# Windows of 80 tokens in the product with v, one subtraction on GpSimd, fewer buffers

## The chip, the cores and the metric

The kernel runs on one core of a Trainium2 chip. The metric is device time in microseconds: the median of the runs, 788.82 us before (788.5 to 789.36, three runs). The profile is that of one execution. TensorE is called PE here, VectorE DVE, ScalarE ACT, GpSimd POOL, as in the profile.

## What is computed

Attention with two mixings of the heads, then two blocks of weights in float64:

```python
# q, k, v: (2, 12, 448, 64); w_pre, w_post: (12, 12)
scores = scale * np.matmul(q, k.transpose(0, 1, 3, 2))
scores = np.einsum('bhij,hg->bgij', scores, w_pre)
scores = scores - np.max(scores, axis=-1, keepdims=True)
attn = np.exp(scores)
attn = attn / (np.sum(attn, axis=-1, keepdims=True) + 1e-09)
attn = np.einsum('bhij,hg->bgij', attn, w_post)
attn = np.matmul(attn, v)
# x: (896, 768), the heads side by side
xn = x / sqrt(mean(x * x, -1) + 1e-6) * rms_g
x = (silu(xn @ w_gate) * (xn @ w_val)) @ w_out      # d_ff 1536
x = elu(x @ w_in2) @ w_out2                         # d_ff 2048
```

## The kernel before

Products that need float32's precision are made of parts: x = h + l, each exact in the format that PE takes. The weights' float64 words are turned into such parts on DVE and ACT (`convert`, L209 to L261), ahead of their use.

The attention works on one batch of 448 tokens after the other. The scores of a head go through DRAM (`s_d`) and come back as groups of ten tokens: 120 partitions hold (token, head), 448 columns the keys. There are 45 groups a batch, 90 in all, here numbered 0 to 89 through both. Each group goes through these steps, on the engine named:

- `g_split`, L468 and L469: high part on ACT, low part `sl` on POOL, for every other group;
- `g_premix`, L476 or L479 to L481: the first mixing of heads, PE;
- `g_max`, L488: the maximum, DVE, from PSUM; `g_exp`, L496: ACT, writes `e` and the sum;
- `g_sum`, L504, and `g_recip`, L511: DVE, one column;
- `g_high`, L524 on ACT or L526 on DVE: the normalised exponentials in float16, `eh`; `g_low`, L533, DVE: what is left of them, `el`;
- `g_postmix`, L554: the second mixing, PE, twelve matmuls with `eh` and `el` as the stationary operand, so that the result comes out with the keys on the partitions;
- `g_out`, L566: ACT copies it into `at`, the room of a window.

A window is some groups in a row. Once its last group has come through `g_out`, PE multiplies its `at` with v (L590), in five pieces, one beside each of the next groups. The result has the features on the partitions and the window's tokens as columns. Then a chain of ten pieces follows, one a step: `squares` (L596 on DVE makes `xt`; L603 to L606 square and add on POOL), `mean` (L612, PE), `root` (L619 on DVE, L623 on POOL), `diagonal` (L627, DVE), `spread` (L631, PE), `normed` (L634, DVE), `high` (L640, ACT, makes `xh`) and `low` (L643, makes `xl`). The last two windows of the second batch are `late`: their squares are made on ACT. `xh` and `xl` feed the first product with the weights.

The order is written out by hand. One loop has a step t for every group; in step t each engine gets, in this order, the work of different groups: on DVE the sum of group t-1, the maximum of t, the reciprocal of t-1, L533 of t-2, L526 of t-1; on PE the premix of t+1 and the postmix of t-3. Beside them stand q, k and scores of later heads, the windows' pieces and the chains' next piece, and near the end the conversion of the first two blocks of weights. So DVE reaches L533 of a group in the step after that in which PE got the postmix of the group two before.

A tile takes the room that its `bufs`-th predecessor of the same tag had, and the first writer waits until the readers of that one are done. Tags that the change touches are `eh` (L522), `el` (L532) and `xt` (L576).

## Time and profile before

| | before |
|---|---|
| median of the runs | 788.82 us |
| span of the profiled execution | 787.3 us |
| busy: PE, DVE, ACT, POOL | 759.4, 550.6, 445.6, 114.4 us |
| attention (to the last `xl` of the second batch) | about 294 us |

The profile gives for each engine the time in which it was busy. Matmuls are pipelined and the ends of their rows are modelled, so starts are the safer reading. PE is nearly full from 294 us to the end; before that different engines are full in different stretches.

### The profile page before, as it was taken

The page shows a single profiled execution, that of the slowest core. Times are in us where ns is not written, and L with a number is a line of the kernel's source. Part 1 is how long each engine was busy: PE and PEld are TensorE (multiplying, and loading weights), DVE is VectorE, ACT ScalarE, POOL GpSimd, SP SyncE. Part 2 cuts the span into 40 slices and gives each one's busy share as a digit, 9 for nine tenths or more (in the row PEclk, how much of TensorE's full clock was granted, in tenths as well). Part 3 has the DMA queues.
Part 4 walks back from the last instruction along what each step waited for, and adds up shares of the span by engine and source line. Part 5 has one row for each costly group of instructions (what it writes and reads, how often), then busy time and mean ns, then how long its engine had stood idle before and what let it go on. Part 6 is the DMA issues. An engine that isn't in the chain of part 4 may idle for free.

```text
span 787.3 us, 14708 instructions
## 1 busy us (share of the span) xinstructions
PE 759.4 (96%) x5655; PEld 673.1 (85%) x5655; DVE 550.6 (70%) x1135; ACT 445.6 (57%) x952; POOL 114.4 (15%) x141
## 2 busy tenths in 40 slices
PE   6779999999998999999999999999999999999997
PEld 5557778777776779999999999999999999999997
DVE  6356999665789938887877865652898887553651
ACT  7679888887987925654544433231576566221320
POOL 4212565333443400000000000000000000000000
PEclk9899999999998999999999999999999999999999
DMA  7798665668783303343332333231444343433512
GB/s 205 222 280 252 168 154 140 178 173 236 217 230 78 104 2 121 122 132 108 121 112 94 116 121 106 95 121 41 121 132 120 109 122 100 111 111 111 155 47 70
DMA packets 90249, 105.42 MB, mean 134 GB/s; under 512 B 16004, under 2 KB 86084, under 8 KB 90180
## 3 DMA queue, kind: packets, MB, share of 16 engines
q1 hardware_dynamic: 90180, 104.49, 46.0%
q8 instruction: 44, 0.72, 0.4%
q14 instruction: 25, 0.20, 0.1%
HBM read 82.46 MB, written 22.02 MB: 133 GB/s over the span
## 4 chain that ended last, share of the span: by engine, by line
PE 83%; DVE 7%; DMA 5%; ACT 2%; issue 1%; SPq 1%; POOL 1%; ACTq 0%; POOLq 0%
PE psa_t L197 13%; PE psa_t L198 13%; PE psa_t L199 13%; PE psv_t L590 5%; PE pst_t L554 4%; PE psf_t L198 4%; PE psf_t L199 4%; PE psf_t L197 4%; PE psa_t L966 3%; PE psa_t L964 3%; PE psa_t L965 3%; DMA s_d<-st 3%; PE psa_t L476 3%; DMA sg<-s_d 2%; PE psa_t L407 2%; DVE el L533 1%
## 5 line engine op out<-in xcount | busy, mean ns | idle before, releaser
L554 PEld LDWEIGHTS <-eh 120*112 120x112 f16 x720 | 66.8, 131 | 27.2 <-issue 21.8
L240 ACT ACTIVATE whl<-w 128x768 fp32r<-128x768 f32 x44 | 37.1, 844 | 86.0 <-PE psf_t L966 28.5
L244 ACT ACTIVATE whl<-w,g_sb 128x128 fp32r<-128x128 f32 x144 | 45.0, 393 | 64.1 <-PE psa_t L199 25.6
L219 ACT ACTIVATE w<-raw 128x768 f32<-128x768 f32 x68 | 62.5, 919 | 30.5 <-DVE whl L251 23.6
L469 POOL TENSOR_TENSOR sl<-sg,sh 120x448 fp32r<-120x448 f32 (+1 forms) x45 | 54.5, 1211 | 116.2 <-ACT sh L468 111.6
L251 DVE TENSOR_TENSOR whl<-w,whl 128x768 fp32r<-128x768 f32 x44 | 42.2, 958 | 41.1 <-ACT whl L240 40.0
L198 PE MATMUL psa_t<-x2l,whl 128*128 128x448 f32 x192 | 70.1, 365 | 0.0
L199 PE MATMUL psa_t<-x2h,whl 128*128 128x448 f32 x192 | 70.1, 365 | 0.0
L197 PE MATMUL psa_t<-x2h,whl 128*128 128x448 f32 x192 | 70.1, 365 | 0.0
L233 DVE SCALAR_TENSOR_TENSOR w<-w,raw 128x768 int32<-128x768 int32 x68 | 65.2, 958 | 2.3
L554 PE MATMUL pst_t<-m2h,eh 120*112 120x120 f16 x360 | 63.0, 217 | 2.7 <-ACT at L566 2.6
L227 DVE SCALAR_TENSOR_TENSOR raw<-raw 128x768 int32<-128x768 int32 x68 | 64.8, 953 | 0.0
L554 PE MATMUL pst_t<-m2h,el 120*112 120x120 f16 x360 | 63.1, 218 | 1.7 <-DVE el L533 1.7
L496 ACT ACTIVATE e<-psa_t,nmax 120x448 f32<-120x448 f32 (+1 forms) x90 | 58.0, 645 | 11.4 <-DVE rs L511 10.4
L533 DVE SCALAR_TENSOR_TENSOR el<-e,rs,eh 120x448 f16<-120x448 f32 (+1 forms) x90 | 64.0, 711 | 0.3 <-ACT eh L524 0.3
L554 PE MATMUL pst_t<-m2l,eh 120*112 120x120 f16 x360 | 63.0, 218 | 0.0
L488 DVE TENSOR_REDUCE nmax<-psa_t 120x1 f32<-120x448 f32 (+1 forms) x90 | 55.2, 613 | 8.4 <-PE psa_t L481 8.3
L197 PE MATMUL psa_t<-xh,whl 128*128 128x448 f32 x150 | 55.7, 372 | 1.0 <-ACT xh L640 1.0
L590 PE MATMUL psv_t<-at,vs 112*64 112x70 f32 (+3 forms) x1344 | 55.7, 230 | 0.0
L590 PEld LDWEIGHTS psv_t<-at,vs 112*64 112x64 f32 x1344 | 46.5, 139 | 9.9 <-issue 7.0
L198 PE MATMUL psa_t<-xl,whl 128*128 128x448 f32 x150 | 54.9, 366 | 0.0
L199 PE MATMUL psa_t<-xh,whl 128*128 128x448 f32 x150 | 54.8, 365 | 0.0
(167 smaller groups left out, 2059.2 us busy)
## 6 DMA issues: line engine op xcount, KB each, us to landing
raw<-in_moe_w_out_dram SPq DMA_DIRECT2D x28, 768.0 KB, 4.5
sg<-s_d SPq DMA_DIRECT2D x44, 420.0 KB, 5.0
s_d<-st SPq DMA_DIRECT2D x93, 196.0 KB, 3.2
raw<-in_moe_w_in_dram SPq DMA_DIRECT2D x16, 768.0 KB, 4.7
raw<-in_moe_w_gate_dram SPq DMA_DIRECT2D x12, 768.0 KB, 4.3
raw<-in_moe_w_val_dram SPq DMA_DIRECT2D x12, 768.0 KB, 4.4
vs<-in_v_dram SPq DMA_DIRECT2D x4, 672.0 KB, 7.7
kt<-in_k_dram SPq DMA_DIRECT2D x12, 224.0 KB, 3.8
```

Of the source, the lines that this page charges most:

```text
L197: nc.tensor.matmul(out=ps, lhsT=wh(kk), rhs=xh_(kk), start=(first and kk == 0), stop=False)
L198: nc.tensor.matmul(out=ps, lhsT=wh(kk), rhs=xl_(kk), start=False, stop=False)
L199: nc.tensor.matmul(out=ps, lhsT=wl(kk), rhs=xh_(kk), start=False, stop=(last and kk == nk - 1))
L219: nc.scalar.activation(out=w, in_=raw.bitcast(F32)[:, :, 1], func=ACTF.Copy, scale=REBASE)
L227: nc.vector.scalar_tensor_tensor(out=lo, in0=hi, scalar=SIGN, in1=lo, op0=ALU.bitwise_and, op1=ALU.bitwise_or)
L233: nc.vector.scalar_tensor_tensor(out=wi, in0=wi, scalar=3, in1=lo, op0=ALU.logical_shift_left, op1=ALU.bitwise_or)
L469: nc.gpsimd.tensor_tensor(out=sl[:r], in0=s32, in1=sh[:r].bitcast(F32), op=ALU.subtract)
L488: nc.vector.tensor_reduce(out=nmax[:r], in_=ps[:r, :S], axis=AXX, op=ALU.max, negate=True)
L496: nc.scalar.activation(out=e32[:r], in_=ps[:r, :S], func=ACTF.Exp, bias=nmax[:r], scale=1.0, accum_out=sm[:r])
L533: nc.vector.scalar_tensor_tensor(out=el[:r], in0=e32[:r], scalar=rs[:r], in1=eh[:r], op0=ALU.mult, op1=ALU.subtract)
L554: nc.tensor.matmul(out=o, lhsT=lhs[:r, c * CP:(c + 1) * CP], rhs=rhs[:r, :, :ni], start=(n == 0), stop=(n == 2),)
L590: nc.tensor.matmul(out=psx[s * D:(s + 1) * D, kk, :n], lhsT=vs[b][:, hh, c, :], rhs=at[:, c, hh, :n], start=(c == 0), stop=(c == NCH - 1),)
```

## The change

Windows now have eight groups (80 tokens), the last of each batch five (48 tokens); there are six a batch and not seven. `low` of a window runs on POOL, but for the two late windows. `eh` has three buffers and not four, `el` two and not three, `xt` two and not three. Comments are left out of the new code, with the lines kept.

```diff
@@ g_high, g_low
-            eh = ap.tile([GP, S], F16, tag="eh", name="eh", bufs=4)
+            eh = ap.tile([GP, S], F16, tag="eh", name="eh", bufs=3)
...
-            el = ap.tile([GP, S], F16, tag="el", name="el", bufs=3)
+            el = ap.tile([GP, S], F16, tag="el", name="el", bufs=2)
@@ windows
-        WGS = [[0, 7, 14, 21, 27, 33, 39, NG], [0, 7, 14, 21, 28, 34, 40, NG]]
+        WGS = [[0, 8, 16, 24, 32, 40, NG]] * B
         NW = len(WGS[0]) - 1
-        WMAX = 70
+        WMAX = 80
@@ window
-            xt = ap.tile([P, KD, WMAX], F32, tag="xt", name="xt", bufs=3)
+            xt = ap.tile([P, KD, WMAX], F32, tag="xt", name="xt", bufs=2)
...
             def low():
-                nc.vector.tensor_tensor(
+                (nc.vector if late else nc.gpsimd).tensor_tensor(
                     out=xl[:, :, tk], in0=xt[:, :, :n], in1=xh[:, :, tk].bitcast(F32), op=ALU.subtract
                 )
```

Tokens of the windows, and the groups (0 to 89) beside whose premix PE gets their five pieces:

| before: tokens | groups | after: tokens | groups |
|---|---|---|---|
| 70 | 12 to 16 | 80 | 13 to 17 |
| 70 | 19 to 23 | 80 | 21 to 25 |
| 70 | 26 to 30 | 80 | 29 to 33 |
| 60 | 32 to 36 | 80 | 37 to 41 |
| 60 | 38 to 42 | 80 | 45 to 49 |
| 60 | 44 to 48 | 48 | 50 to 54 |
| 58 | 50 to 54 | | |
| 70 | 57 to 61 | 80 | 58 to 62 |
| 70 | 64 to 68 | 80 | 66 to 70 |
| 70 | 71 to 75 | 80 | 74 to 78 |
| 70 | 78 to 82 | 80 | 82 to 86 |
| 60 | 84 to 88 | 80 (late) | behind 89 |
| 60 (late) | behind 89 | 48 (late) | behind 89 |
| 48 (late) | behind 89 | | |

DVE in the second batch, from `g_low` of group 68 on, shortly before the first block of weights is converted (L643 is `low`, L619 the start of `root`, L596 the first multiplication of a window). Before:

```order
L533 SCALAR_TENSOR_TENSOR el<-e_3969,rs,eh 120x448
L643 TENSOR_TENSOR xl<-xt,xh 128x6x70
L504 TENSOR_SCALAR sm<-sm 120x1
L488 TENSOR_REDUCE nmax<-psa_t 120x1
L511 RECIPROCAL rs<-sm 120x1
L533 SCALAR_TENSOR_TENSOR el<-e_4016,rs,eh 120x448
L526 TENSOR_SCALAR eh<-e_4048,rs 120x448
L619 TENSOR_SCALAR ms<-psa_t 70x1
```

After:

```order
L533 SCALAR_TENSOR_TENSOR el<-e_3881,rs,eh 120x448
L596 TENSOR_TENSOR xt<-psv_t,vsc 128x480
L504 TENSOR_SCALAR sm<-sm 120x1
L488 TENSOR_REDUCE nmax<-psa_t 120x1
L511 RECIPROCAL rs<-sm 120x1
L533 SCALAR_TENSOR_TENSOR el<-e_3931,rs,eh 120x448
L526 TENSOR_SCALAR eh<-e_3968,rs 120x448
L504 TENSOR_SCALAR sm<-sm 120x1
```

The subtraction L643 is gone from this queue; the window's first multiplication L596, which stood five steps further on, or two earlier for the window before, stands in its place.

POOL at the same place (L469 is `sl` of the premix, L603 to L606 the squares, L623 the root). Before:

```order
L623 TENSOR_TENSOR rstd<-ms,mhalf 70x1
L469 TENSOR_TENSOR sl<-sg,sh 120x448 x2
L603 TENSOR_TENSOR sq<-xt 128x420
L604 TENSOR_TENSOR sq<-sq 128x210
L605 TENSOR_TENSOR sq<-sq 128x70
L606 TENSOR_TENSOR sq<-sq 128x70
L469 TENSOR_TENSOR sl<-sg,sh 120x448 x2
L623 TENSOR_TENSOR rstd<-ms,mhalf 70x1
```

After:

```order
L606 TENSOR_TENSOR sq<-sq 128x80
L469 TENSOR_TENSOR sl<-sg,sh 120x448
L643 TENSOR_TENSOR xl<-xt,xh 128x6x80
L469 TENSOR_TENSOR sl<-sg,sh 120x448
L623 TENSOR_TENSOR rstd<-ms,mhalf 80x1
```

L643 now stands between two subtractions of the premix's parts, and ahead of the next root.

PE in the first batch, at group 42 (L554 is the postmix, L476 the next group's premix), where the old order had the last piece of a window of 60 tokens and the new one is between two windows:

```order
 L554 LDWEIGHTS el
 L554 MATMUL pst_t<-m2h,el 112x120
-L590 MATMUL psv_t<-at,vs 64x60 x8
 L476 MATMUL psa_t<-sg,m1f 120x448
 L554 LDWEIGHTS eh
```

The premix now follows the postmix directly.

## Rows read from the trace of the kernel before

**Rows 1.** The page's head: the length of the profiled execution.

```profile
span 787.3 us, 14708 instructions
```

**Rows 2.** Stretch, length, busy us of PE, PEld, DVE, ACT, POOL; clock, DMA, GB/s.

```profile
60.00:82.00 22.00, 21.94 (x246) 16.37 (x247) 15.23 (x45) 21.24 (x53) 5.38 (x6) 1.00 0.82 239
82.00:107.00 25.00, 22.10 (x285) 18.07 (x284) 24.30 (x55) 19.79 (x50) 17.18 (x21) 1.00 0.71 167
107.00:184.00 77.00, 76.84 (x1002) 60.71 (x1000) 59.13 (x166) 64.88 (x154) 34.08 (x41) 1.00 0.63 165
184.00:196.00 12.00, 11.44 (x132) 8.66 (x127) 6.98 (x20) 8.09 (x20) 3.52 (x5) 1.00 0.90 245
196.00:226.00 30.00, 30.00 (x354) 23.29 (x353) 22.00 (x64) 28.18 (x69) 12.90 (x16) 1.00 0.78 221
226.00:266.00 40.00, 36.90 (x487) 29.74 (x487) 39.55 (x97) 32.68 (x80) 17.48 (x19) 0.91 0.54 150
266.00:293.60 27.60, 26.56 (x401) 22.31 (x397) 13.78 (x41) 13.86 (x33) 6.07 (x9) 1.00 0.01 2
293.60:780.00 486.40, 486.35 (x2494) 458.79 (x2495) 338.39 (x571) 214.46 (x405) 0.00 (x0) 1.00 0.36 108
```

**Rows 3.** By line and form, count | busy us, mean ns: product with v.

```profile
L590 PE MATMUL psv_t<-at,vs 112*64 112x70 f32 x672 | 29.2, 234 | 0.0
```

**Rows 4.** Chain that ended last (start us, us, what): that product's pieces.

```profile
67.30 1.12 PE psv_t L590 x32
...
70.45 0.64 PE psv_t L590 x16
...
131.69 0.61 PE psv_t L590 x16
...
139.13 1.08 PE psv_t L590 x32
...
283.08 1.49 PE psv_t L590 x48
```

**Rows 5.** By line and form: spreading a window's norm.

```profile
L631 PE MATMUL psa_t<-dg,ones 70*128 70x70 f32 x14 | 2.7, 274 | 0.9 <-DVE sm L504 0.9
```

**Rows 6.** DVE's lines from 226 to 266 us.

```profile
L533 DVE SCALAR_TENSOR_TENSOR el<-e,rs,eh 120x448 f16<-120x448 f32 x15 | 11.2, 749 | 0.0
...
L255 DVE SCALAR_TENSOR_TENSOR whl<-w,g_sb,whl 128x128 fp32r<-128x128 f32 x12 | 5.3, 509 | 0.0
L526 DVE TENSOR_SCALAR eh<-e,rs 120x448 f16<-120x448 f32 x5 | 4.0, 796 | 0.0
...
L643 DVE TENSOR_TENSOR xl<-xt,xh 128x420 fp32r<-128x420 f32 x3 | 1.8, 584 | 0.0
L627 DVE TENSOR_SCALAR dg<-ident,rstd 70x70 f32<-70x70 f32 x2 | 1.4, 686 | 0.0
```

**Rows 7.** DVE in order of time: start us, us, instruction.

```profile
227.54 0.58 DVE L643 TENSOR_TENSOR xl<-xt,xh 128x420 fp32r<-128x420 f32 x1
228.05 0.14 DVE L504 TENSOR_SCALAR sm<-sm 120x1 f32<-120x1 f32 x1
```

**Rows 8.** By line and form: GpSimd's subtraction for the premix.

```profile
L469 POOL TENSOR_TENSOR sl<-sg,sh 120x448 fp32r<-120x448 f32 x44 | 53.3, 1212 | 110.7 <-ACT sh L468 106.2 <-PE psa_t L481 4.3
```

**Rows 9.** L526, L533 (min/median/max ns) and L255 over the run, one L627.

```profile
L526 DVE TENSOR_SCALAR eh<-e,rs x40: 439/449/2019, 40.9 to 250.7; 120x448 f16<-120x448 f32 x39, 96x448 f16<-96x448 f32 x1
...
L533 DVE SCALAR_TENSOR_TENSOR el<-e,rs,eh x90: 654/667/1232, 42.6 to 275.5; 120x448 f16<-120x448 f32 x88, 96x448 f16<-96x448 f32 x2
...
L255 DVE SCALAR_TENSOR_TENSOR whl<-w,g_sb,whl 128x128 fp32r<-128x128 f32 x144 | 43.8, 363 | 12.1 <-ACT whl L244 12.1
...
254.50 0.25 DVE L627 TENSOR_SCALAR dg<-ident,rstd 70x70 f32<-70x70 f32 x1
```

**Rows 10.** In order of time: one L533, and a postmix matmul.

```profile
250.08 0.67 DVE L533 SCALAR_TENSOR_TENSOR el<-e,rs,eh 120x448 f16<-120x448 f32 x1
...
249.87 0.31 PE L554 MATMUL pst_t<-m2h,el 120*112 120x120 f16 x1
```

## The prediction

> **What bounds the kernel now.** I read the busy time by stretch first, with cuts where the nearly full engine changes [rows 2]. From 293.6 us to 780 TensorE (PE) has 486.35 of 486.40 us: the three products with the weights, which the change doesn't touch and which simply start earlier or later. So everything is decided in the attention, up to 293.6 us. There the bound wanders. From 60 to 82 us ScalarE has 21.24 of 22 us. From 82 to 107 VectorE (DVE) has 24.30 of 25, while q and k of the second batch are prepared. From 107 to 184 and from 196 to 226 PE has all but 0.2 us. From 184 to 196 nobody is full: a DMA stall after v of the second batch is loaded. From 226 to 266 DVE has 39.55 of 40 us, because the first two blocks of weights are converted beside the groups; PE has 36.90, of which some at half clock (granted 0.91 on average, against 1.00 around it). From 266 to 293.6 PE has 26.56 of 27.6. A saving counts only where its engine is the full one: PE's in 107 to 226 and after 266, DVE's in 82 to 107 and 226 to 266. What ScalarE does is unchanged but for two copies of a window.
>
> **Product with v on PE.** A window is 48 products in the code, each two records, since 7 windows of 70 rows give 672 [rows 3]. They come in one piece of 32 records and four of 16. At 70 rows the pieces take 1.12 and 0.64 us, at 60 rows 1.08 and 0.61 [rows 4]; a window is 1.12 + 4 x 0.64 = 3.68, or 1.08 + 4 x 0.61 = 3.52. At 48 rows 48 records took 1.49, which is 31 ns a record and not less than at 60 rows (1.08 / 32 = 34, with a start-up of about 0.14 in it). [...] For 80 rows the bounds are the line through 60 and 70 (0.67 and 1.16, window 3.84) and everything in proportion to the columns (0.73 and 1.28, window 4.20). [...]
>
> All windows before: 7 x 3.68, four of 3.52, one of 60 rows in three long pieces (3.24), 58 rows 3.5, 48 rows 3.1: 49.7 us. After: nine of 4.09, one in three long pieces 3.75, 48 rows 3.45 and 3.1: 47.1. PE loses 2.6 us of work (3.8 to 1.5 at the bounds). But where? In PE's order, numbering the groups 0 to 89 through both batches, the premixes of groups 28 to 69 (the stretch to 226 us in which PE is full) had three pieces of 0.64, three windows of 3.52, one of 3.5 and two of 3.68 between them: 23.3. Now there are four windows of 4.09, one of 48 rows (3.45) and four pieces of the next (1.25 + 3 x 0.71 = 3.38): 23.2. Only 0.1 us falls out there, and one spread of the norm (L631, 2.7 / 7 = 0.39 us a window, [rows 5]), say 0.35. From group 85 on, four pieces of 0.61, 3.24 and 3.1 become two of 0.71, 3.75 and 3.1: 0.5 less. The other 2 us leave groups 16 to 27 and 70 to 84, where DVE is the full engine, and become idle time of PE. Sum for PE: **-1.0 us**.
>
> **The norm's chain on DVE, 226 to 266 us.** Three subtractions of the low part (L643) stand there, 0.58 us each, of which the next instruction sees 228.05 - 227.54 = 0.51 [rows 6, 7]. They leave DVE: -1.53. In DVE's order the 15 groups from 70 on also lose one of two multiplications by the norm (L634; same 420 elements, so 0.5), which now stands just behind the stretch; I count half, -0.25. Three operations that stay grow from 420 to 480 elements, 60 more at 1 ns (0.58 us for 420 bounds it at 1.4): +0.18. Together -1.6.
>
> Against it stand two of the moved subtractions, now on GpSimd (POOL). The nearest row is the subtraction of the premix's parts, 448 elements in 1212 ns [rows 8]; 480 elements make 1.30 us. POOL is busy 17.48 of the 40 us there [rows 2], and while it works DVE is slow: five L526 took 4.0 us where the median of one is 0.449, 15 L533 took 11.2 where it is 0.667, twelve L255 had a mean of 509 ns against 363 over the run, two L627 a mean of 686 where the shorter took 0.25 [rows 6, 9]. That is 1.8 + 1.2 + 1.8 + 0.9 = 5.7 us lost to 17.48 us of POOL, a third. Two times 1.30 by a third: +0.85. Bounds are nothing (0) and the whole 1.30 of each (+2.6). **-0.75 us**, between -1.6 and +1.0.
>
> **82 to 107 us.** By the order, groups 17 to 25 lose one L643 and gain one first multiplication of a window (xt), which has moved by a step: nothing. On average they must gain a little, 9 groups of 0.07; one subtraction on POOL falls on the end of the stretch. **-0.2 us**, between -0.7 and +0.6.
>
> **Fewer buffers.** With two buffers for el, the subtraction L533 of a group must wait until PE has done the postmix of the group two before; for eh the same wait stands one instruction later. In the trace this was nearly always over. I paired all 90: the one case in the DVE-bound stretches that would have waited is L533 at 250.08, where the last L554 of that postmix ends at 249.87 + 0.31 = 250.18 [rows 10]: 0.1 us. Premix and postmix stand back to back on PE, and DVE first takes the maximum of that premix, so the wait is met by construction; what would queue behind it on DVE is the next eh and the window's pieces. With two buffers of xt the older is read for the last time nine steps after it is written, and wanted again after thirteen or more. I count 0. **Tail:** the last window but one is 80 rows, not 60: four operations 60 to 120 elements longer before the last xl, **+0.2**.
>
> Sum: -1.0 - 0.75 - 0.2 + 0.2 = -1.75 us. The profiled span is 787.3 [rows 1], 1.5 us under the median of 788.82, which lies around the span; so 785.6 of span, **787.1 us**. A measurement of this kernel can tell about 0.2% (1.6 us) from no change, so the forecast sits just beyond that line.
>
> [...]
>
> **Rivals.** (1) *GpSimd blocks DVE in full.* Three moved subtractions lie where DVE is full (about groups 26, 71, 79). If each catches an L526 or a row of L255 it costs not a third but 1.3 to 1.57 us (2019 - 449), 3.9 to 4.7 together where I had counted 1.3; from 1.0 us each on the gain is gone, and from 1.55 on the kernel is measurably slower. With the worst, and 0.5 for a step elsewhere in which DVE is nearly full, 787.1 + 3.4 + 0.5 = 791. For it: the slow L526 rows. [...] (2) *Nothing arrives.* DVE's relief is eaten and PE's is idle time: 788.6. For it: the 2 us of PE work that fall out in the wrong stretches. (3) *More arrives.* DVE already loses 5.7 us to POOL from 226 to 266; the squares of the windows shift by one to seven steps and may leave the L255 rows alone, and a shorter stretch may spare PE the half clock: 2 to 3 us more, 784.5. (4) *The rings of el and eh couple DVE to PE.* If every group waits 0.3 us from 226 to 266, 15 x 0.3 = +4.5: 791.6. Against it, the paired times.
>
> **How the numbers follow.** Forecast (-0.5 to -3 us) 50%, of it 30 beyond -0.2%; more arrives 18%; nothing 15%; blocked 13%; rings 4%. Faster 0.48, same 0.35, slower 0.17. The range runs from 784.0 (the low ends of POOL's cost and half of rival 3) to 790.0 (POOL's upper end with the PE gain lost); beyond it lie some 2 in 10.
>
> **What would show it.** Right: from about 226 us a DVE-bound stretch shorter by about 1 us with no L643 in it, PE pieces of 0.71 and 1.25, L533 nearly never waiting for L554. Wrong: L526, L533 or L255 with larger means than before beside L643 on POOL; pieces under 0.68; a wait of L533 on PE; a DMA stall that grows, or a change after 293 us, which I exclude.

## The result, and the profile after

| | before | after |
|---|---|---|
| median of the runs | 788.82 us | 798.21 us (794.38 to 800.31, five) |
| profiled execution, and its span | span 787.3 us | 794.38 us, span 792.7 us |
| busy: PE, DVE, ACT, POOL | 759.4, 550.6, 445.6, 114.4 us | 756.7, 552.5, 444.8, 121.7 us |
| last `xl` written | 294.1 us | 299.3 us |
| from there to the end of the span | 493.3 us | 493.3 us |

The change is slower: 1.0109 times before, 95% interval 1.0083 to 1.0135. The forecast was 787.1 us, in a range from 784.0 to 790.0. In this document ratios leave out executions that are over 1.5% above the fastest of their kernel (three of the twelve of e1, one of e2, two of e3 below), and medians count them. The profiled execution is the shortest of the five and explains only the 5.3 us by which its attention ends later. A second profile of the same kernel, of an execution of 801.24 us (h0 below), ends its attention at 298.8 us and then takes 500.7 us instead of 493.3, in code that the change doesn't touch. So there are two losses, and they lie in different places.

The busy time by stretch, of the change, answers to [rows 2]; columns are the stretch, its length, busy us of PE, PEld, DVE, ACT and POOL, granted clock, DMA share, GB/s:

```profile
82.00:107.00 25.00, 21.91 (x280) 18.23 (x280) 24.36 (x54) 19.61 (x49) 14.62 (x17) 1.00 0.63 149
107.00:184.00 77.00, 74.41 (x880) 59.10 (x879) 59.77 (x152) 63.73 (x152) 37.61 (x43) 0.98 0.64 165
184.00:196.00 12.00, 12.00 (x137) 9.15 (x135) 7.40 (x22) 7.71 (x19) 4.54 (x6) 1.00 0.91 239
196.00:226.00 30.00, 28.00 (x314) 21.29 (x313) 20.15 (x55) 27.37 (x67) 12.55 (x14) 1.00 0.76 217
226.00:266.00 40.00, 35.40 (x413) 27.37 (x410) 39.42 (x89) 29.98 (x73) 19.38 (x19) 0.91 0.50 134
266.00:299.30 33.30, 30.91 (x433) 25.99 (x431) 17.57 (x50) 19.22 (x45) 9.66 (x11) 1.00 0.12 40
299.30:785.00 485.70, 485.59 (x2492) 458.27 (x2492) 337.82 (x571) 213.27 (x404) 0.00 (x0) 1.00 0.36 108
```

VectorE still bounds 82 to 107 and 226 to 266 us, as forecast. What is new is the second row: from 107 to 184 us, where PE had 76.84 of 77 us, it now has 74.41, and its granted clock is 0.98 and not 1.00. From 196 to 226 it has 28.00 of 30. PE has become idle in the stretches that it used to bound.

The product with v by itself costs what was forecast. In the chain that ended last (start, us, what), one long piece and a short one of a window of 80:

```profile
117.01 1.26 PE psv_t L590 x32
120.44 0.70 PE psv_t L590 x16
```

1.25 and 0.71 stand in the forecast's sum. PE's busy time over the whole run fell by 759.4 - 756.7 = 2.7 us, where 2.6 was said. DVE's busy time rose by 1.9 us, although ten L643 of some 0.58 us [rows 6] had left it. L533 alone takes 7.7 us more: its busy time and mean over the run, first before, then the change:

```profile
L533 DVE SCALAR_TENSOR_TENSOR el<-e,rs,eh 120x448 f16<-120x448 f32 (+1 forms) x90 | 64.0, 711 | 0.3 <-ACT eh L524 0.3
```

```profile
L533 DVE SCALAR_TENSOR_TENSOR el<-e,rs,eh 120x448 f16<-120x448 f32 (+1 forms) x90 | 71.7, 796 | 1.3 <-PE pst_t L554 0.9
```

One place at which PE stands idle is L612, the two matmuls that sum a window's squares: by line and form, busy and mean, then the idle time just ahead and what ended it. First before, then the change:

```profile
L612 PE MATMUL psa_t<-ones,sq 128*70 128x2 f32 x14 | 1.9, 202 | 1.6 <-DVE par L386 1.4 <-POOL sq L606 0.2
```

```profile
L612 PE MATMUL psa_t<-ones,sq 128*80 128x2 f32 x18 | 2.4, 205 | 5.7 <-POOL sq L606 2.8 <-DVE sm L504 2.4 <-ACT e L496 0.6
```

PE waits 5.7 us there and not 1.6, half of it for the last sum of squares on GpSimd (L606). By the starts of L612, 2.4 us of it lie at 91 us and 0.9 at 256, in stretches that VectorE fills; 0.6, 0.7 and 1.1 lie at 112, 157 and 277 us, where PE was the full engine before. At 111 us PE's order of time is this (start, us, instruction, idle time before it):

```profile
111.78 0.27 PE L612 MATMUL psa_t<-ones,sq 128*80 128x2 f32 x2 [0.58 <-ACT e L496]
113.33 1.85 PE L476 MATMUL psa_t<-sg,m1f 120*120 120x448 f32 x2 [1.28 <-DVE sm L504]
```

The same two microseconds in the table by stretch, with the two behind them:

```profile
110.00:112.00 2.00, 1.42 (x20) 1.28 (x18) 2.00 (x6) 1.73 (x6) 1.84 (x4) 1.00 1.11 215
112.00:114.00 2.00, 0.72 (x2) 0.48 (x2) 2.00 (x6) 0.87 (x3) 2.00 (x3) 0.83 1.17 211
114.00:116.00 2.00, 2.00 (x13) 1.24 (x12) 2.00 (x5) 1.55 (x4) 0.79 (x2) 0.50 0.30 77
```

PE is busy 0.72 of 2 us, then the granted clock falls from 1.00 to 0.50, and the 13 matmuls of the next 2 us fill them. In before PE had 2.00 of 2 us in each of these. But VectorE, too, has 2.00 of 2 us in all three rows, and the longer of the two waits, 1.28 us, is the premix's for VectorE's L504. So PE is idle here because VectorE is late as well: just before, at 111.36 us, an L526 beside L643 takes 1.38 us for a median of 0.45.

On VectorE, the place at which the loss in the second batch arises (DVE first, then POOL, start and us):

```profile
256.18 1.21 DVE L533 SCALAR_TENSOR_TENSOR el<-e,rs,eh 120x448 f16<-120x448 f32 x1
257.32 1.56 DVE L224 TENSOR_SCALAR w<-w 128x768 f32<-128x768 f32 x1
258.80 1.88 DVE L227 SCALAR_TENSOR_TENSOR raw<-raw 128x768 int32<-128x768 int32 x1
```

```profile
256.88 1.59 POOL L643 TENSOR_TENSOR xl<-xt,xh 128x480 fp32r<-128x480 f32 x1
258.57 1.30 POOL L469 TENSOR_TENSOR sl<-sg,sh 120x448 fp32r<-120x448 f32 x1
```

L643 takes 1.59 us here and 1.20 at 156.65 us, where it meets no long operation of VectorE. L533 takes 1.21 (median 0.667, [rows 9]) and L224, a scaling by a constant, 1.56, where it takes 0.56 in the middle of its 68:

```profile
L224 DVE TENSOR_SCALAR w<-w x68: 549/560/1564, 238.7 to 763.2; 128x768 f32<-128x768 f32 x68
```

The longest L533 of the change is held up by L643 itself (DVE, then POOL):

```profile
199.72 2.07 DVE L533 SCALAR_TENSOR_TENSOR el<-e,rs,eh 120x448 f16<-120x448 f32 x1
```

```profile
200.09 1.21 POOL L643 TENSOR_TENSOR xl<-xt,xh 128x480 fp32r<-128x480 f32 x1
```

It ends 0.48 us behind L643. So does each of the L533 that take over 0.76 us, 15 in before and 20 in the change: it ends 0.48 us behind the end of an instruction that ran on GpSimd beside it, most often one of the squares or L469. The holding goes both ways: the four L643 of 1.58 to 1.59 us began while such an L533 was under way, and each ends some 1.06 us behind it.

### The profile page after: what moved, and what is told of

The parts are those of the page before. It is cut to its first block, busy times and chain, and to the rows that moved or that the text cites. A ratio compares the mean times of both kernels' runs of the same rounds, so it can differ in the third digit from the quotient of the medians.

```text
span 792.7 us, 14340 instructions
## 1 busy us (share of the span) xinstructions
PE 756.7 (95%) x5455; PEld 671.6 (85%) x5455; DVE 552.5 (70%) x1115; ACT 444.8 (56%) x950; POOL 121.7 (15%) x141
## 4 chain that ended last, share of the span: by engine, by line
PE 82%; DVE 7%; DMA 4%; ACT 3%; issue 2%; POOL 1%; SPq 1%; POOLq 0%; ACTq 0%
PE psa_t L197 12%; PE psa_t L198 12%; PE psa_t L199 12%; PE pst_t L554 5%; PE psv_t L590 4%; PE psf_t L197 4%; PE psf_t L198 4%; PE psf_t L199 4%; PE psa_t L964 3%; PE psa_t L965 3%; PE psa_t L966 3%; PE psa_t L476 3%; DMA s_d<-st 2%; DVE el L533 2%; PE psa_t L407 2%
## 5 line engine op out<-in xcount | busy, mean ns | idle before, releaser
L554 PEld LDWEIGHTS <-eh 120*112 120x112 f16 x720 | 68.0, 133 | 26.6 <-issue 19.8
L533 DVE SCALAR_TENSOR_TENSOR el<-e,rs,eh 120x448 f16<-120x448 f32 (+1 forms) x90 | 71.7, 796 | 1.3 <-PE pst_t L554 0.9
L469 POOL TENSOR_TENSOR sl<-sg,sh 120x448 fp32r<-120x448 f32 (+1 forms) x45 | 54.0, 1199 | 114.8 <-ACT sh L468 100.0
L554 PE MATMUL pst_t<-m2h,el 120*112 120x120 f16 x360 | 64.1, 221 | 3.3 <-DVE el L533 3.2
L554 PE MATMUL pst_t<-m2h,eh 120*112 120x120 f16 x360 | 64.3, 219 | 1.6 <-ACT at L566 1.4
L554 PE MATMUL pst_t<-m2l,eh 120*112 120x120 f16 x360 | 64.3, 219 | 0.0
L488 DVE TENSOR_REDUCE nmax<-psa_t 120x1 f32<-120x448 f32 (+1 forms) x90 | 55.2, 613 | 8.3 <-PE psa_t L481 8.0
L566 ACT ACTIVATE at<-pst_t 112x480 f32<-112x480 f32 (+1 forms) x90 | 52.3, 581 | 3.8 <-PE pst_t L554 3.3
L964 PE MATMUL psa_t<-whl,gh 128*128 128x384 f32 x160 | 53.4, 334 | 0.0
```

Source lines behind the costliest of these rows:

```text
L469: nc.gpsimd.tensor_tensor(out=sl[:r], in0=s32, in1=sh[:r].bitcast(F32), op=ALU.subtract)
L488: nc.vector.tensor_reduce(out=nmax[:r], in_=ps[:r, :S], axis=AXX, op=ALU.max, negate=True)
L533: nc.vector.scalar_tensor_tensor(out=el[:r], in0=e32[:r], scalar=rs[:r], in1=eh[:r], op0=ALU.mult, op1=ALU.subtract)
L554: nc.tensor.matmul(out=o, lhsT=lhs[:r, c * CP:(c + 1) * CP], rhs=rhs[:r, :, :ni], start=(n == 0), stop=(n == 2),)
L964: nc.tensor.matmul(out=o, lhsT=gh[:, kk, tk], rhs=wh[:, j], start=first, stop=False)
```

## The experiments

For the runs with a profile the table gives where the attention stands: the start of the maximum (L488) of groups 48 and 89, the last `xl`, and what follows to the end of the span.

| kernel | median us (ratio to before, 95%) | span | group 48 | group 89 | last `xl` | rest |
|---|---|---|---|---|---|---|
| before | 788.8 | 787.3 | 166.5 | 272.4 | 294.1 | 493.3 |
| the change | 798.2 (1.0083 to 1.0135) | 792.7 | 167.5 | 277.3 | 299.3 | 493.3 |
| e1 | 796.5 (1.0048 to 1.0104) | 787.4 | 165.6 | 272.5 | 294.1 | 493.3 |
| e2 | 791.8 (1.0020 to 1.0054) | 792.8 | 166.5 | 277.1 | 299.5 | 493.3 |
| e4 | 794.5 (1.0049 to 1.0101) | 791.9 | 167.3 | 275.0 | 297.0 | 494.9 |
| f1, f2 (as e1) | one each: 795.9, 792.4 | 794.2, 790.7 | 168.6, 168.8 | 276.2, 275.8 | 299.3, 297.4 | 494.9, 493.3 |
| e3 | 788.6 (0.9980 to 1.0038) | 784.8 | 164.4 | 269.8 | 291.5 | 493.3 |
| f3 | 789.0 (0.9981 to 1.0007) | 787.2 | 166.7 | 272.3 | 293.9 | 493.3 |
| f4 | 788.4 (0.9980 to 1.0021) | 789.4 | 166.7 | 273.7 | 296.1 | 493.3 |
| g1 | 793.7 (1.0047 to 1.0085) | 791.2 | 168.3 | 276.2 | 298.0 | 493.3 |
| g2 | 792.5 (1.0029 to 1.0088) | 789.5 | 162.9 | 273.2 | 296.2 | 493.3 |
| g3 | 795.9 (1.0065 to 1.0121) | 793.4 | 167.5 | 275.7 | 299.0 | 494.5 |
| g4 | 792.9 (1.0037 to 1.0103) | 789.9 | 162.5 | 273.6 | 296.5 | 493.4 |
| h0 (the change) | one: 801.2 | 799.5 | 166.9 | 276.8 | 298.8 | 500.7 |
| h1 | 798.6 (1.0087 to 1.0139) | 798.2 | 163.6 | 276.2 | 297.5 | 500.7 |
| h2 | 798.4 (1.0098 to 1.0182) | 803.2 | 168.7 | 277.4 | 301.0 | 502.1 |
| h3 | 794.1 (1.0041 to 1.0077) | 791.8 | 166.6 | 276.9 | 298.6 | 493.3 |
| j1 | 793.6 (1.0027 to 1.0095) | 788.5 | 161.3 | 271.7 | 293.9 | 494.6 |

A profile is one execution; where it and the median differ, the text says so.

### The low part on GpSimd

e1 takes the change and puts L643 back on VectorE; e2 takes before and puts it on GpSimd; e4 takes the change and starts it a step later. Beside L643 the change has two L526 of 1.38 and 1.40 us, an L220 of 1.57 and an L224 of 1.56, where the medians are 0.45, 0.56 and 0.56.

```diff
# e1, on the change
-                (nc.vector if late else nc.gpsimd).tensor_tensor(
+                nc.vector.tensor_tensor(
# e2, on before
-                nc.vector.tensor_tensor(
+                (nc.vector if late else nc.gpsimd).tensor_tensor(
# e4, on the change
-            chain = [squares, None, mean, root, None, diagonal, spread, normed, high, low]
+            chain = [squares, None, mean, root, None, diagonal, spread, normed, high, None, low]
```

> The changed kernel with the subtraction L643 back on DVE; windows of 80 and the smaller rings stay. [...] Theory B (two buffers of el and three of eh make DVE wait for PE): still 793 to 799. Theory C (pieces of 80 columns are too long for PE): still 793 to 799, with pieces of L590 well over 0.71 and 1.25 us.

> The kernel before with one edit: L643 of the windows that are not late runs on POOL; windows of 70 and 60 and the larger rings stay. [...] Theories B and C: 788 to 789.5, as before.

> The changed kernel with the subtraction on POOL one step of the loop later. [...] Theories B and C: 796 to 800, the same DVE rows.

e2 is the price of the move alone: 0.37% (0.20 to 0.54), some 3 us, with windows and buffers as before. Its 791.8 us lie between the 788 to 789.5 expected if the buffers or the long pieces cost the time and the 793 to 801 expected if the move does. In its profile, of an execution of 794.5 us, the attention ends 5.4 us later. 1.7 of these arise between groups 56 and 60, where ScalarE's L418 waits 5.0 us for a store of scores and not 3.3 as in before; no run ties that to the low part. From group 70 to 85, where VectorE is full, it loses 2.0. So the move alone is a loss, and not the gain of 0.75 us that was forecast. e4's median is 3.7 us less than the change's, and its attention ends 1.8 to 2.3 us before those of the change's two profiles, so the step at which the subtraction starts matters; but it stays 0.75% over before. That the cost depends on which instruction of VectorE the subtraction meets held in part: L643 meets no L526 there any more, but still an L220 and an L224, which take 1.56 us each. e1 is the surprise. If the move were the loss, 786.5 to 789.5 was expected; with L643 back on VectorE the kernel is still 1.0076 times before, and its twelve executions run from 789.1 to 802.9 us. The profiled one, the shortest, ends its attention at 294.1, as before; f1 and f2 below are longer ones.

### The buffers

```diff
# e3, on before: all three. f3: the first two alone. f4: the third alone
-            eh = ap.tile([GP, S], F16, tag="eh", name="eh", bufs=4)
+            eh = ap.tile([GP, S], F16, tag="eh", name="eh", bufs=3)
-            el = ap.tile([GP, S], F16, tag="el", name="el", bufs=3)
+            el = ap.tile([GP, S], F16, tag="el", name="el", bufs=2)
-            xt = ap.tile([P, KD, WMAX], F32, tag="xt", name="xt", bufs=3)
+            xt = ap.tile([P, KD, WMAX], F32, tag="xt", name="xt", bufs=2)
```

> The kernel before with one edit: eh 3, el 2, xt 2 buffers. [...] Theory B: 793 to 799, with a wait of L533 on L554 of some us in sum.

> The kernel before with the rings of the exponentials' parts cut (high parts 4 to 3, low parts 3 to 2) and the xt ring left at 3. Theory that these rings cause the spread seen with all three cut (4 of 12 executions at 795 to 800): here too about a third of the executions lie over 794, median 788 to 789. Theory that the xt ring causes it: none over 793, median 786 to 787.

> The kernel before with the ring of xt cut from 3 to 2 and the rings of the exponentials as before. Theory that the exponentials' rings cause the spread: no execution over 793, median 788 to 789. Theory that the xt ring causes it: about a third over 794. A third theory, that the room of the pool and with it the addresses of its buffers decides: both single cuts show the spread, or neither.

None of the three differs from before. In the change itself L533 waits 0.9 us for PE's L554 over the whole run. e3 has a spread, though: eight executions from 786.5 to 791.8 and four from 795.2 to 800.0, against none of twelve over 791.5 in f3 and one, 796.1, in f4. What a longer execution looks like, f1 and f2 were to show:

> The changed kernel with the low part back on VectorE, as in e1, for one more profiled execution: its executions went from 789.1 to 802.9, and the one profiled so far was the shortest. If the length comes from the rings of exponentials, an execution of about 797 shows it between 60 and 300 us, in VectorE's L533 or L526 waiting for TensorE's L554 more often than the 0.9 us of the change's profile, and the last stretch stays 493.3. If it comes from the matmuls' clock, the granted clock is below .988 and the last stretch, with nothing changed in its code, is longer than 493.3 by most of the excess.

> The same kernel once more, since 8 of its 12 executions were over 794. Expected as for the run before it: a long one shows its excess over e1's 787.4 us of span either in the attention, at a ring, or in the last stretch, at the clock.

Neither expectation held as it was put. The excess over e1 arises in lots of 0.7 to 1.5 us at several places of the attention, and no ring is among them; 0.7 to 0.8 us of it is there at group 12, ahead of the first window's product, and in f1 1.6 lie behind the attention. In e1, f1 and f2 alike PE lies nearly idle around 89 us (0.05, 0.23 and 0.35 us busy from 88 to 90); in f1 and f2, not in e1, its clock falls behind that, to 0.50 from 92 to 94 us against 1.00. Four windows of 2 us of f2:

```profile
88.00:90.00 2.00, 0.35 (x4) 0.14 (x2) 2.00 (x3) 1.37 (x3) 1.80 (x2) 1.00 0.89 241
90.00:92.00 2.00, 1.27 (x8) 0.86 (x9) 2.00 (x7) 0.73 (x3) 0.00 (x0) 0.92 0.78 130
92.00:94.00 2.00, 2.00 (x23) 1.90 (x24) 2.00 (x7) 1.42 (x3) 0.55 (x1) 0.50 0.46 103
94.00:96.00 2.00, 2.00 (x32) 1.88 (x29) 1.16 (x4) 1.09 (x4) 1.75 (x2) 0.73 0.71 173
```

### The steps without a piece of the product

A window's product comes in five pieces, one a step. With windows of seven groups two steps of seven have none; with eight groups it is three of eight, and just in these steps the window's mean (L612) waits on PE. So the number of pieces was changed and nothing else.

```diff
# g1, on before
-            return [... for k0, k1 in ((0, 2), (2, 3), (3, 4), (4, 5), (5, 6))]
+            cuts = [0, 2, 3, 4, 5, 6] if late else [0, 2, 4, 5, 6] if n == WMAX else [0, 2, 4, 6]
+            return [... for k0, k1 in zip(cuts, cuts[1:])]
# g2 on e1, g3 on before, g4 on the change
+            cuts = [0, 2, 3, 4, 5, 6] if late else [0, 1, 2, 3, 4, 5, 6]
+            return [... for k0, k1 in zip(cuts, cuts[1:])]
```

> The kernel before with each window's product with v in 4 pieces instead of 5 (in 3 for windows of 60), so that 3 steps of a window's 7 have no piece, as 3 of 8 have in the change. Clock theory: in the traces of the change and of e1, TensorE lies idle for 1.3 to 2 us at about 88 to 91 and 111 to 113 us, where a window has no piece, and the granted clock falls to .50 for some 3 to 5 us right behind, in the stretch that TensorE bounds; the trace of before has no such fall there. With 3 steps without a piece the falls come here too, between 85 and 180 us, and the median is 790 to 795. Rival, that 80-row windows or smaller rings do it some other way: nothing falls there and the median stays 788 to 790.

> e1 (the change with the low part on VectorE) with the product with v in 6 pieces, one pair of heads each, so that 2 steps of 8 have none instead of 3. Clock theory: fewer or shorter falls of the granted clock between 85 and 120 us than in e1 and its two looks (4 falls in three profiles); median 787 to 791 instead of 796.5, and a narrower spread. Rival (rings, rows of 80): median and spread as e1, 795 to 798.

> The kernel before with 6 pieces instead of 5. Its windows of 70 then have one step without a piece and those of 60 none. Clock theory: no fall between 60 and 230 us, as before; the time is the same or shorter by what the fall at 240 to 250 us costs, 786 to 789. If the later start of a window's chain costs more than that, 789 to 791.

> The change itself with 6 pieces instead of 5, low part on GpSimd. If the clock explains what is wrong beside the low part, the median falls from 798 to what the low part on GpSimd alone costs over before (e2: ratio 1.0037, 791.8): 790 to 794. If the low part on GpSimd is the main cost by itself, it stays at 796 to 799.

g1 makes of before what the change made of it: three steps without a piece, and 4.9 us more, as its clock theory said (790 to 795). Its loss arises from group 27 to 70 (3.2 us) and behind group 85 (3.0). Ahead of that PE goes idle at 98 us (0.44 of 2 us busy) and its clock falls behind to 0.50, where before has neither:

```profile
98.00:100.00 2.00, 0.44 (x7) 0.30 (x4) 2.00 (x3) 1.90 (x5) 1.77 (x4) 1.00 0.83 207
100.00:102.00 2.00, 1.66 (x13) 1.22 (x14) 2.00 (x7) 0.49 (x1) 1.42 (x2) 0.87 0.80 185
102.00:104.00 2.00, 2.00 (x15) 2.00 (x14) 2.00 (x7) 1.96 (x6) 0.72 (x1) 0.50 0.00 0
```

g4 is the change with two such steps and not three: 5.3 us less (792.9 against 798.2), and at group 48 it is 5.0 us ahead of the change and 4.0 ahead of before. Its attention ends 2.3 to 2.8 us before those of the change; the rest of the 5.3 between the medians may be the longer pace that is told below. g2 does the same for e1 and comes to 792.5, between its two forecasts. So the windows of 80 can bring what was hoped of them, and more, if the product is spread over the steps. Both give it back later (below). g3 was expected at 786 to 789 and came to 795.9, a miss: with windows of six groups the sixth piece meets the next window, and its first matmul then waits for VectorE to empty the one buffer of the result:

```profile
L590 PE MATMUL psv_t<-at,vs 112*64 112x60 f32 x480 | 20.4, 229 | 3.3 <-DVE xt L596 2.9 <-DVE sm L504 0.4
```

That is a new wait and tells nothing on the clock.

### The wait, or the clock behind it

Most losses up to here went with a fall of PE's clock, so the falls could be the cause; against it, e1's profile has falls at 112 us (0.57) and 252 us (0.53) and an attention as short as before's. h1 takes the wait at L612 away by starting the mean a step later; h2 leaves it and gives PE 32 small matmuls ahead of it in three windows; h3 does the like in before, ahead of its fall at 243 us.

```diff
# h1, on the change, behind the line of the chain
+            if not late:
+                chain.insert(1, None)
# h2, on the change; h3, on before
+        bank = {}
+        def keep_busy(k):
+            for _ in range(k):
+                nc.tensor.matmul(
+                    out=bank["v"][:D, 480:512], lhsT=ident[:, :D], rhs=ident[:, :32], start=True, stop=True
+                )
...
-            psx = psv.tile([P, KD, WMAX], F32, tag="v", name="psv_t")
+            bank["v"] = psv.tile([P, 512], F32, tag="v", name="psv_t")
+            psx = bank["v"][:, :KD * WMAX].rearrange("p (k t) -> p k t", k=KD)
...
# h2, in mean()
+                if (b, w) in ((0, 0), (0, 1), (1, 2)):
+                    keep_busy(32)
# h3, in the loop over the groups, ahead of g_premix
+            if 71 <= t <= 76:
+                keep_busy(16)
```

> The change with the mean of each window's squares one step later, the last two windows as they were. In the change's trace TensorE stands 5.7 us at L612 (1.6 in before), 2.8 of it for the last sum on GpSimd (L606), with the premix that VectorE needs queued behind. If this wait is what lets TensorE fall idle and its clock fall, the wait at L612 drops below 2 us, the fall at 112 is gone and the median is 791 to 795. If the steps without a piece of the product are enough for it, TensorE idles there anyway, the falls stay and the median is 796 to 799.

> The change with 32 matmuls of 32 columns that nobody reads ahead of the mean in three windows, at about 88, 111 and 257 us, where TensorE stands idle in the change's trace. They take some 1 to 2 us each out of TensorE's idle time and free nothing earlier. If the falls of the clock cost the time, the ones at 112 and 256 (or 90) are gone and the median is 792 to 796, though there is more work; if the idle time itself or VectorE's longer operations cost it, the median is 798 to 801.

> The kernel before with 16 such matmuls in each of six steps, at about 228 to 242 us, where VectorE sets the pace and TensorE has gaps; in the trace of before its clock falls to .50 from 242 to 252 us behind them. If a fall costs its time even in a stretch that VectorE bounds, the median is 785 to 787.5 (faster than before by 1.5 to 3 us); if it costs nothing there, 788 to 790, and if the matmuls hold up the premix, 790 to 792.

h2 takes the fall at 112 us away, as these rows show, and at 256 us too (1.00 from 256 to 260 us, where the change has 0.50 to 0.67):

```profile
112.00:114.00 2.00, 2.00 (x35) 1.94 (x33) 2.00 (x3) 0.66 (x2) 1.62 (x3) 1.00 1.06 220
114.00:116.00 2.00, 2.00 (x38) 2.00 (x36) 1.83 (x5) 2.00 (x6) 1.81 (x2) 1.00 0.88 141
```

Nothing is won by it. Compared with the change's profile, h2 has lost 1.1 us more by group 27, since its matmuls outlast the gap, and from there on runs step for step like it: over the fall, from group 27 to 30, the change loses 1.1 us against before and h2 1.3, and from 30 to 48 both win back 0.7. If the fall had cost, h2 would catch up there. (It has falls of its own later, at 278 and 302 us.) h3 says the same of before: the fall at 243 to 250 us is gone (granted 1.00 from 240 to 250 us, 0.66 in before), and from group 76, just ahead of it, to group 89 h3 runs step for step like before, 4.4 to 4.6 us behind. Its own cost, at 794.1 above all three of its forecasts, is that its matmuls hold up the premixes: VectorE has 11.86 of 14 us from 226 to 240 where it had all 14.

```profile
226.00:240.00 14.00, 14.00 (x244) 12.99 (x242) 11.86 (x28) 8.39 (x21) 5.03 (x4) 1.00 0.61 166
```

So the clock theory fell in these stretches, which VectorE fills in the change and in before: the falls mark where PE was idle, and taking them away gave nothing back. Where PE is the bound it is otherwise: in e4, f1, g3 and j1 a fall lies between 292 and 304 us, as in this row of j1,

```profile
292.00:298.00 6.00, 4.93 (x16) 4.25 (x17) 4.51 (x9) 2.53 (x7) 0.00 (x0) 0.72 0.01 2
```

and their rest is 494.5 to 494.9 us and not 493.3. A fall there costs 1.2 to 1.6 us.

Nor does the wait at L612 by itself explain the loss. h1 has no idle time left ahead of it in the windows of 80,

```profile
L612 PE MATMUL psa_t<-ones,sq 128*80 128x2 f32 x18 | 2.4, 203 | 0.0
```

and at group 48 it is 3.3 to 3.9 us ahead of the two profiles of the change, of which 0.9 to 1.5 were there at group 12, ahead of any window. Its median is the change's all the same, above the 791 to 795 that were expected without the wait. Half of the lead is gone by group 63, at the DMA stall behind the loading of v, where PE has 1.22 of the 4 us from 190 to 194 and waits 2.3 us at the L612 of the window of 48, for ScalarE's L418; at the last group 0.6 to 1.1 us are left, after two L643 of 1.59 us in the second batch's busy stretch. And its profiled execution took 500.7 us behind the attention, as h0's, which the next section is about.

### The stretch that the change doesn't touch

> The change itself once more, for a second profiled execution: the one profiled was its shortest, 794.4, where the median is 798.2. Clock theory: a longer one has more or other falls of the granted clock to .50, above all outside 30 to 60 us, than the four of the profile (34 to 40, 54 to 60, 112 to 118, 256 to 264); one of them may lie behind 293 us, in a stretch whose code is that of before (g3: 298 to 302, with 1.2 us more behind the attention). Rival: the same falls, and the excess at GpSimd, with VectorE's operations beside L643 longer still.

h0 has as many falls as the first profile, one of them elsewhere, and its attention ends 0.5 us earlier. What makes it 6.8 us longer lies behind, where PE is never idle. One line of the products with the weights, 400 to 600 us, in the first profile and then in h0:

```profile
L198 PE MATMUL psa_t<-ul,whl 128*128 128x448 f32 x144 | 52.6, 365 | 0.0
```

```profile
L198 PE MATMUL psa_t<-ul,whl 128*128 128x448 f32 x144 | 53.0, 368 | 0.0
```

A matmul of 448 columns starts 202.7 ns after the one before it in the one and 206.7 ns in the other (the mean distance of starts, from 300 to 690 us), at a granted clock of 1.00 in both. The rows show how it begins, the change's first profile and then h0, each from its last wait on:

```profile
298.89 0.47 PE L197 MATMUL psa_t<-xh,whl 128*128 128x448 f32 x1 [1.02 <-ACT xh L640]
...
299.76 0.36 PE L199 MATMUL psa_t<-xh,whl 128*128 128x448 f32 x1
...
301.18 0.37 PE L197 MATMUL psa_t<-xh,whl 128*128 128x448 f32 x1
```

```profile
298.40 0.47 PE L197 MATMUL psa_t<-xh,whl 128*128 128x448 f32 x1 [1.02 <-ACT xh L640]
...
299.27 0.36 PE L199 MATMUL psa_t<-xh,whl 128*128 128x448 f32 x1
...
300.92 0.37 PE L198 MATMUL psa_t<-xl,whl 128*128 128x448 f32 x1
```

Seven matmuls in 1.42 us, eight in 1.65. Some 1,840 such matmuls follow without a wait; 4 ns each are 7.3 us, which is all but 0.1 of the difference of 493.3 and 500.7. All three profiles of executions over 797 us (h0, h1, h2) have the longer distance, and none of the sixteen under 796 us. To see whether the pace belongs to an execution or is taken up at a wait, i1 puts 13 short pauses into the stretch.

```diff
# on the change, in run(), behind a unit's matmuls
+        if out and u % 3 == 2:
+            for _ in range(2):
+                nc.tensor.matmul(out=out[-1][:16, 448:464], lhsT=scr, rhs=scr, start=True, stop=True)
+                nc.gpsimd.memset(scr, 0.0)
```

> The change with 13 short pauses of TensorE behind the attention: a matmul of 16 columns, a fill of its operand on the idle GpSimd, and the same matmul again, which waits for that fill. Nothing of the output depends on it. In the profiles so far the matmuls of 448 columns behind 300 us start 202.7 ns apart in fifteen executions and 206.7 ns apart in three (two of longer ones of the change's own kind among them), from the last wait at 298 us to some 690 us without a break, at a granted clock of 1.00 in both; that is 7.4 us. Theory that the way TensorE comes out of its last wait decides the pace and that it keeps it until it waits again: the pace changes at some of the pauses within one execution, and the twelve times lie between the short and the long ones, around 797 to 800 plus the pauses' own 5 to 10 us, closer together than 794 to 801. Theory that something of the whole execution decides it (addresses, the chip's state): one pace from 300 to 690 us in spite of the pauses, and times in two groups 7 us apart.

A pause is a wait of 0.23 us:

```profile
338.75 0.21 PE L823 MATMUL psf_t<-scr 128*16 128x16 f32 x2 [0.23 <-POOL scr L824]
```

The same line of the product between four of the pauses, 317 to 337, 340 to 360, 386 to 406 and 409 to 429 us:

```profile
L200 PE MATMUL psf_t<-xl,whl 128*128 128x448 f32 x21 | 7.7, 368 | 0.0
```

```profile
L200 PE MATMUL psa_t<-xl,whl 128*128 128x448 f32 x22 | 8.0, 365 | 0.0
```

```profile
L200 PE MATMUL psa_t<-xl,whl 128*128 128x448 f32 x21 | 7.7, 368 | 0.0
```

```profile
L200 PE MATMUL psf_t<-xl,whl 128*128 128x448 f32 x22 | 8.0, 365 | 0.0
```

The pace changes at the pauses, to and fro within one execution: of 14 stretches those behind the first, fourth, seventh, ninth and twelfth pause run at 206.7 ns and the others at 202.6 or 202.7. That is every third pause as long as the stretches between them are equally long, so the pace is not left to chance there; what decides it is not shown. The five times lie within 807.9 to 811.5 us, closer than the change's own. So in i1 the pace is taken up when PE comes out of a wait and kept until it waits again. One profile shows another occasion. In h2 four matmuls behind the last wait take 0.81 us, the short pace (the long one makes 0.83),

```profile
301.44 0.36 PE L199 MATMUL psa_t<-xh,whl 128*128 128x448 f32 x1
...
302.25 0.51 PE L197 MATMUL psa_t<-xh,whl 128*128 128x448 f32 x1
```

then the granted clock falls to 0.50 until 305.7 us, and behind the fall they start 206.7 ns apart. (Behind the falls of e4, f1, g3 and j1 they start 202.7 ns apart.) Behind 299 us the change has no wait on PE to the end, and so one event decides 7.4 us.

### A version that keeps the lead

> The kernel of g2 (the change's windows and rings, low part on VectorE, six pieces) with five pieces again in the last two windows of the first batch and the last three of the second. In g2's trace the attention is 3.5 us ahead of before at group 48; in g4's TensorE then waits 1.5 us at L590 for the load of v, which the later last piece issues later, and behind the last group g2 loses another 1.3 us. If these two waits cost what g2 gives back, the attention ends at 291 to 293 us (before 294.1) and the span is 784.5 to 786.5 in an execution at 202.7 ns a matmul behind it, some 7 us more at 206.7; median 786.5 to 789 with some times 7 us above. Rival: the falls of the clock go elsewhere and take it back, end at 295 to 297 us, median 791 to 793 as g2.

```diff
# on g2
-            cuts = [0, 2, 3, 4, 5, 6] if late else [0, 1, 2, 3, 4, 5, 6]
+            cuts = [0, 2, 3, 4, 5, 6] if w >= NW - 2 - b else [0, 1, 2, 3, 4, 5, 6]
```

j1 is 5.2 us ahead of before at group 48, 1.1 of it since group 12, ahead of the first window's product, and, unlike g2 and g4, still 4.4 at group 52, so the load of v was what they lost there. From group 60 to 64 it loses 1.4 and behind group 80 another 2.4, and the last `xl` comes at 293.9, level with before and between its two forecasts; the median, 793.6, is above both. Six of its times lie from 788.9 to 791.6 and six from 795.7 to 800.0. No kernel here is faster than before by more than can be told.

## Why the prediction was wrong, step by step

By the starts of L488 the attention falls into the stretches of the sum. Forecast, and difference from before in us:

| stretch | forecast | the change, h0 | e1, f1, f2 | e2 |
|---|---|---|---|---|
| up to group 27 | -0.2 | +0.6, 0.0 | 0.0, +2.1, +2.3 | +0.4 |
| group 27 to 70 (PE full before) | -0.45 | +1.8, +1.7 | -0.5, +0.1, +0.4 | +1.3 |
| group 70 to 85 (VectorE full) | -0.75 | +1.9, +2.1 | -0.6, +0.3, -0.6 | +2.0 |
| group 85 to the last `xl` | -0.3 | +1.0, +1.0 | +1.2, +2.7, +1.2 | +1.7 |

Up to group 12 no window has reached PE, and the profiles differ by up to 1.3 us from before there already, so the first row is the least certain.

- **What bounds the kernel.** The stretches of VectorE were read rightly (24.36 of 25 and 39.42 of 40 us after). The step that failed is "PE's in 107 to 226 and after 266", as stretches in which PE's work alone sets the time. From group 27 to 70 PE has 2.0 us less to do and idles 4.6 us where it idled 0.7; behind group 85 it waits 1.1 us for L606. No term of the sum priced such waits. 2.4 of the 5.7 us at L612 are among them; the others there are 1.8 us for VectorE (1.3 at 113 us, 0.5 for L533's `el`) and 1.5 for ScalarE's L418, which itself waits 4.4 us for a store and not 3.3, so "a DMA stall that grows" came true as well. Windows of eight groups leave three steps without a piece of the product, which was read as work saved. g1 shows in before that fewer pieces cost time just here (3.2 and 3.0 us), and in g4 more pieces give a lead of 4 us by group 48. But h1, without the wait at L612 in the windows of 80, still loses 1.5 us from group 27 to 70, so how this loss divides between missing cover and a late VectorE is not shown.
- **Product with v on PE.** Right in size: 1.26 and 0.70 us a piece, 2.7 us less in all. The sum is added up from 4.09 us for a window of 80 (0.71 and 1.25 a piece), an estimate of the author's between the bounds of 3.84 and 4.20; no run shows it, and in the change a window takes 1.26 + 4 x 0.70 = 4.06. (Of the bounds for the whole, 3.8 should be 5.1: nine windows of 3.84 and one of 3.48.) Its "-1.0 us" of effect did not arrive in the change; in j1, with the low part on VectorE and six pieces, the lead over before grew by 4.1 us from group 12 to 48, more than was said, and was lost again by the end.
- **The norm's chain on DVE.** The term of -0.75 us had the wrong sign: from group 70 to 85 the change and e2 lose 1.9 to 2.1 us, and the kernels with L643 on VectorE do not. The "third" was a mean over everything that POOL does, taken at equal parts on whatever VectorE runs. L643 on POOL took 1.58 us and not 1.30 where an L533 was under way, and met instructions that it held up: beside it one L526 took 1.38 us for a median of 0.45, one L224 1.56 for 0.56. e2 puts the move at 3 us. That is rival 1, which had 13% and 791; e2's median is 791.8. The L224 and the L526 beside L643 lasted until it was through (they end 0.4 and 0.2 us behind it), and so did the L533 of 2.07 us, which ends 0.48 behind it. L533's median of 667 ns in before [rows 9] is no sign against that: its long ones there, the worst of 1232 ns among them, all end 0.48 us behind an instruction of GpSimd. The median says only that few met one. By what means GpSimd holds VectorE up is not shown.
- **Fewer buffers at 0.** Right: 1.0009, 0.9994 and 1.0001, with before inside every interval, and rival 4 fell with it (0.9 us of wait in the whole run).
- **After 293 us.** "A change after 293 us, which I exclude" is the second step that failed. The work there is unchanged and PE is full in both, but busy is not a rate: it took 493.3 us in one profile of the change and 500.7 in the other, and these 7.4 us hang on how PE leaves its last wait.
- **Rival 2 and 3.** Neither came. "A shorter stretch may spare PE the half clock" was besides worth nothing: h2 and h3 took falls to 0.50 away in such stretches and won no time.

The median's 9.4 us are then some 5 us of attention (5.3 and 4.8 in the two profiles) and the longer pace behind it in part of the executions. Within the attention the parts don't add up: e2 alone loses 5.4 us of attention in its profile and 3 in the median, e1 alone 0, 3.3 and 5.2 in three profiles, both together 5. A rival that no run tests alone is that the windows of 80 shift GpSimd's work, the squares above all, to where it holds VectorE: summed over its median, L533 loses 4.0 us in before, 11.6 in the change, but also 9.3 in e1, where L643 is not on GpSimd; two of 1.97 and 2.05 us stand at 84 and 88 us in the change, where VectorE is full. Why the longer pace came so often with the change and e1 and seldom in before (three of 123 executions over 795 us), and whether all unprofiled long executions have it, stays open. So does what made e3's four long ones.

## What to carry to other kernels

Work that stands beside a wait on an engine can be cover, and a coarser tiling thins it out, here to three bare steps of eight, with 5.7 us of wait at L612 for 1.6: count the steps that lose it, not only the time saved. Price contention between two engines by the instructions that will actually stand side by side, worst case included (here an L224 of 1.56 us for 0.56), and not by an average over all that ran. Whether an instruction was held showed here in where it ends (0.48 us behind GpSimd's), not in the median of its kind (0.667 us in before and in the change). A stretch that one engine fills to 100% can still change its length, as this one did from 493.3 to 500.7 us: compare the distance of its instructions' starts, over more than one profiled execution, before calling it untouched.

## What the runs showed of the hardware that was not expected

- The same stream of matmuls (128 rows, 448 columns, float32r, each with its own load of weights) has two paces at full granted clock, 202.7 and 206.7 ns from start to start. In i1 the pace changes at waits as short as 0.23 us and not between them; in h2 it changed over a fall of the granted clock.
- A granted clock of 0.50 for some microseconds behind an idle PE cost no time that could be seen in the attention, where VectorE set the pace (h2, h3), and 1.2 to 1.6 us just behind it, where PE did (e4, f1, g3, j1).
- Every L533 that took over 0.76 us, 15 in before and 20 in the change, ends 0.48 us behind the end of an instruction of GpSimd. The longest took 2.07 us for a median of 0.667.
- GpSimd's subtraction of two times 480 float32 elements a partition takes 1.20 to 1.21 us, and 1.58 to 1.59 where an L533 was under way when it began and ended ahead of it; a VectorE scaling beside it stretches from 0.56 to 1.56 us.
